# Finer pieces at both ends, small products on GpSimd, and more of TensorE's waits in the plan of an attention and FFN kernel

## The chip, the cores and the metric

The kernel runs on one core of a Trainium2 chip. The metric is the device time of one execution in microseconds. The core has five engines that run side by side, each in the order in which its instructions were written: TensorE (PE) multiplies matrices into PSUM, ScalarE (ACT) computes activations, VectorE (DVE) does arithmetic on tensors, GpSimd (POOL) does arithmetic on SBUF only, and SyncE (SP) issues DMAs. PEld is TensorE's load of weights, which has rows of its own in the profile.

## The reference, cut to what matters

Sizes: S = 2048 rows, D = 512, H = 32 heads of 16, F = 1792; data in bf16.

```
g = sigmoid((x * gate_w).sum(-1, keepdims=True))
q, k, v = split(x @ wqkv)                       # 32 heads of 16
a = concat(softmax(q @ k.T * 16**-0.5) @ v) @ wo
b = (silu(x @ w_gate) * (x @ w_up)) @ w_down
out = g * a + (1 - g) * b
```

## The kernel before, in words

**Tiles.** The queries are cut into 4 blocks of 512 (qb), the heads into 8 groups of 4 (g). One block with one group is a unit, 32 in all (UNIT, line 117), and a unit has 16 key tiles of 128. One key tile of a unit, in the text a tile, has 4 heads, so it is four score banks of 128 keys x 512 queries in PSUM: 512 tiles, 2048 banks. The 8 PSUM banks are shared by all work.

**Two ways to an exponential.** A score bank becomes a probability either on ScalarE (`emit_group`: one ACTIVATE with Exp over two banks, sometimes three, into `e_all`), or on VectorE (`emit_d`): a TENSOR_SCALAR turns the fp32 score into the bits of a number (tile `c_t`, or a home in `wd_t` or `kaug`), and further cheap operations on the whole 2048 columns of the tile improve it. These are either two bit operations and one product (`bits`, `product`, group size 2) or three shifted copies (`copy`, group size 4). GpSimd takes over some of the copies and of the products in pieces (`lifted`, `beside`, `take_over`). Each result is a moving operand of the multiplication with v (`pv`), so a tile of VectorE costs TensorE two or four such multiplications, and one of ScalarE one.

**The order is written out by a planner.** The Python code that emits the instructions keeps a clock for each engine (`Plan`: pe, dve, act, pool), advances it by fixed costs (`spend` for TensorE, `spend_v` for VectorE), and picks the next instruction by scores whose weights stand in `WEIGHTS`, changed at about 60 given slots of the run. The split of the tiles between ScalarE and VectorE comes out of the same choice (`choose`, `v_unit`). The chip does not see the plan, only the order on each engine and the semaphores between engines. `later` queues work for VectorE, and `fill_dve` decides when it goes out; the flag `fast` marks operations that read SBUF only. `beside(span)` gives GpSimd work when the next operations of VectorE read PSUM; a dependency ties each such GpSimd instruction behind the last `fast` VectorE instruction before it.

**Side work** (qkv projections, the FFN, output projections) comes in chains of pieces (`Chain`, `Pacer`), each with a release slot and a deadline; `force` empties a chain that is due. `q_pieces` makes the query operand of two groups: a copy out of PSUM (`qst`), its magnitude `aq`, the product of `aq` with the bound of the keys `kb` (`weigh`), and 2 x 8 DMAs on the SP queue.

**End of a unit.** `post` copies the sum over the keys out of PSUM into `osb` and adds a tiny number to the denominators' rows. `settle` sends the rows to `onc` and the denominators to DRAM. `recip`, once for each query block, loads the denominators as `dn`, inverts them, spreads them as `rb` by DMA, and multiplies each of the blocks of `onc` by `rb` (`norm`; 4 blocks for the first three query blocks, 3 for the last).

**Both ends.** At the start (from line 1560 on) the first keys (`kp0`, two banks) and queries (`qp0`) are projected; the largest key magnitude (`largest`, `k_neg`) makes a bound that is added to the queries (`bound_add`), and two masked variants of the queries (`q0a`) feed the first scores. At the end the last unit's sum is copied by ScalarE, its denominators are collected (`denominators`), inverted, spread over the rows (`spread_rows`), multiplied in (`on_l`), and the last product with wo goes into four banks (`a_ps`) that already hold the rest of the output; `last_pieces` and `tail` make that rest.

## Time and profile before

| | us |
|---|---|
| median of 3 runs | 751.14 (750.82 to 751.19) |
| profiled execution, its time | 751.17 |
| span from its first to its last instruction | 749.4 |
| first exponential of scores begins | 13.44 |
| last exponential of scores ends | about 740.6 |

The profile comes from one execution. All positions in it are microseconds from the start of the span, and 1.77 us of the profiled execution lie outside it. The helpers record all instructions of TensorE under line 260, of ScalarE under 263 and of VectorE, GpSimd and SP under 275, so groups are told apart by their tiles. The busy time of a group counts an overlap of two instructions of one engine once, and the mean is of single instructions, which overlap their neighbours: two VectorE instructions of 0.68 us each can begin 0.60 us apart. The spacing of the beginnings is what an instruction costs its engine.

### The profile page before, as it was taken

The page shows a single profiled execution, that of the slowest core. Times are in us where ns is not written, and L with a number is a line of the kernel's source. Part 1 is how long each engine was busy: PE and PEld are TensorE (multiplying, and loading weights), DVE is VectorE, ACT ScalarE, POOL GpSimd, SP SyncE. Part 2 cuts the span into 40 slices and gives each one's busy share as a digit, 9 for nine tenths or more (in the row PEclk, how much of TensorE's full clock was granted, in tenths as well). Part 3 has the DMA queues.
Part 4 walks back from the last instruction along what each step waited for, and adds up shares of the span by engine and source line. Part 5 has one row for each costly group of instructions (what it writes and reads, how often), then busy time and mean ns, then how long its engine had stood idle before and what let it go on. Part 6 is the DMA issues. An engine that isn't in the chain of part 4 may idle for free.

```text
span 749.4 us, 23683 instructions
## 1 busy us (share of the span) xinstructions
PE 733.1 (98%) x10009; PEld 237.0 (32%) x10009; DVE 724.2 (97%) x1196; ACT 733.5 (98%) x827; POOL 246.2 (33%) x342
## 2 busy tenths in 40 slices
PE   7999999999999999999999999999999999999997
PEld 3333332333332333333333233233333333332332
DVE  6799999999999999999999999999999999999995
ACT  5999999999999999999999999999999999999996
POOL 5142030442534443531443322553113403403221
PEclk9999999999999999999999999999999999999999
DMA  9000212344210003220200041312000231200001
GB/s 211 23 2 16 51 32 42 72 121 101 49 36 13 20 24 82 58 53 21 59 16 11 25 109 31 70 27 60 18 23 16 62 82 42 47 19 14 14 31 36
DMA packets 91025, 34.48 MB, mean 46 GB/s; under 512 B 75488, under 2 KB 90472, under 8 KB 90920
## 3 DMA queue, kind: packets, MB, share of 16 engines
q1 hardware_dynamic: 89192, 32.66, 18.5%
q8 instruction: 78, 1.28, 0.7%
q10 hardware_dynamic: 1728, 0.33, 0.3%
q14 instruction: 27, 0.22, 0.1%
HBM read 21.55 MB, written 2.35 MB: 32 GB/s over the span
## 4 chain that ended last, share of the span: by engine, by line
ACT 70%; PE 24%; DVE 4%; issue 2%; DVEq 0%
ACT e_all L263 66%; PE psum L260 24%; ACT th L263 3%; DVE c_t L275 2%; DVE mt L275 0%; DVE gs L275 0%; DVE kaug L275 0%; ACT mt L263 0%; ACT xT L263 0%; DVE rd L275 0%; ACT osb L263 0%; DVE osb L275 0%; DVE o_t L275 0%; DVE qx L275 0%; DVE rn L275 0%
## 5 line engine op out<-in xcount | busy, mean ns | idle before, releaser
L263 ACT ACTIVATE e_all<-psum 128x1024 bf16<-128x1024 f32 x758 | 709.7, 1126 | 1.2 <-PE psum L260 1.0
L275 DVE TENSOR_SCALAR c_t<-psum 128x512 uint16<-128x512 f32 x443 | 295.4, 686 | 4.4 <-PE psum L260 3.3
L260 PE MATMUL psum<-qx,kaug 32*128 32x512 bf16 (+1 forms) x1632 | 250.3, 385 | 6.0 <-ACT e_all L263 4.4
L275 POOL TENSOR_TENSOR c_t<-c_t,lift 128x256 int32<-128x256 int32 (+2 forms) x152 | 105.7, 702 | 274.5 <-DVE c_t L275 216.3
L260 PE MATMUL psum<-e_all,vaug 128*32 128x512 bf16 (+3 forms) x2032 | 169.5, 330 | 0.0
L260 PEld LDWEIGHTS <-kaug 32*128 32x128 bf16 (+1 forms) x2048 | 76.3, 91 | 268.8 <-ACT e_all L263 195.7
L260 PEld LDWEIGHTS <-vaug 128*32 128x32 bf16 x4012 | 96.8, 95 | 125.1 <-issue 88.4
L260 PE MATMUL psum<-c_t,vaug 128*32 128x512 bf16 (+3 forms) x1712 | 132.9, 337 | 0.5 <-DVE mt L275 0.2
L275 DVE TENSOR_SCALAR c_t<-c_t 128x2048 uint16<-128x2048 uint16 (+1 forms) x191 | 129.8, 686 | 0.9
L275 POOL TENSOR_TENSOR c_t<-c_t 128x512 bf16<-128x512 bf16 (+2 forms) x54 | 49.7, 933 | 84.8 <-DVE c_t L275 45.8
L260 PE MATMUL psum<-wd_t,mt 128*32 128x512 bf16 x896 | 73.4, 382 | 0.0
L260 PE MATMUL psum<-xT,wg 128*32 128x512 bf16 x896 | 72.6, 384 | 0.0
L260 PE MATMUL psum<-xT,wu 128*32 128x512 bf16 x896 | 71.7, 383 | 0.4 <-DVE c_t L275 0.3
L275 DVE TENSOR_TENSOR c_t<-c_t 128x2048 bf16<-128x2048 bf16 (+1 forms) x42 | 50.9, 1213 | 0.0
L260 PE MATMUL psum<-q,kaug 32*128 32x512 bf16 (+1 forms) x256 | 50.1, 385 | 0.5 <-ACT e_all L263 0.2
L275 DVE TENSOR_SCALAR kaug<-psum 128x512 uint16<-128x512 f32 (+1 forms) x67 | 44.8, 687 | 0.8 <-PE psum L260 0.4
L260 PE MATMUL psum<-xT,wqk 128*32 128x512 bf16 x512 | 40.9, 383 | 0.0
L263 ACT ACTIVATE th<-psum 128x512 bf16<-128x512 f32 x56 | 38.8, 693 | 0.0
L275 DVE SCALAR_TENSOR_TENSOR gs<-th,psum 128x512 bf16<-128x512 bf16 x56 | 37.9, 676 | 0.4 <-ACT th L263 0.3
L275 DVE SCALAR_TENSOR_TENSOR mt<-gs,psum 128x512 bf16<-128x512 bf16 x56 | 37.9, 677 | 0.3
L275 POOL TENSOR_TENSOR kaug<-c_t,lift 128x256 int32<-128x256 int32 (+1 forms) x31 | 21.1, 681 | 50.3 <-DVE c_t L275 33.2
L275 POOL TENSOR_TENSOR c_t<-kaug,lift 128x256 int32<-128x256 int32 (+1 forms) x30 | 20.7, 697 | 40.1 <-DVE c_t L275 19.7
(124 smaller groups left out, 464.0 us busy)
## 6 DMA issues: line engine op xcount, KB each, us to landing
wg<-in_B_w_gate_dram SPq DMA_DIRECT2D x56, 128.0 KB
wu<-in_B_w_up_dram SPq DMA_DIRECT2D x56, 128.0 KB
on<-osb SPq DMA_DIRECT2D x120, 16.0 KB
rb<-rr SPq DMA_DIRECT2D x15, 128.0 KB
wd_t<-in_B_w_down_dram SPq DMA_DIRECT2D x7, 256.0 KB
qx<-qst SPq DMA_DIRECT2D x96, 16.0 KB
qx<-aq SPq DMA_DIRECT2D x96, 16.0 KB
out_dram<-o_t SPq DMA_DIRECT2D x12, 128.0 KB
```

Of the source, the lines that this page charges most:

```text
L260: return ordered(nc.tensor.matmul(out, lhsT=lhsT, rhs=rhs, **kw), [lhsT, rhs], [out])
L263: ordered(nc.scalar.activation(out=out, in_=in_, **kw), [in_, *kw.values()], [out])
L275: return ordered(f(*a, **kw), [v for v in (*a, *kw.values()) if v is not out], [out])
```

## The change

Five groups of edits.

**Start.** The keys' projection runs bank by bank instead of alternating, each bank has its own maximum (`largest(0)`, `largest(3)`) and its own copy to `kaug`; the queries are made in two halves of 256 columns in two banks (`qp0` and `warm`), and VectorE evicts the one half while ScalarE evicts the other.

**GpSimd.** `weigh` (16 products) and `norm` of the first three query blocks (12 products) are made by GpSimd in pieces of 256 columns, through a new list `asides` that `beside` serves ahead of the tile's own work. The tiny number is added to `dn` once for each query block, by GpSimd (a new list `guarded`, on which `spread` waits); so `post` makes a plain copy for 29 of the 32 units.

**Planner.** New constants for TensorE (FLIP, UNIT_US, PIECE_US, COLS_US, TURN); score groups begin no earlier than the query chain's planned end, multiplications with v no earlier than their operands' planned ends, the `parts` chain no earlier than its ratio. These alter the order only, they add no semaphore.

**Weights.** EB, FACE, OWN, LATEST and all entries of `WEIGHTS` have new values, with LATEST as a 27th of each entry.

**End.** The last unit's copy, denominators, inversion and spreading go in two halves; the rest of the output is made by four chains of five column pieces, one for each 128 rows (`last`), which the pacer can place from 8, 6, 4 and 2 slots before the end.

The diff, without the weights:

```diff
-    FLIP, UNIT_US, PIECE_US, COLS_US = 0.097, 0.224, 0.011, 0.213
+    FLIP, UNIT_US, PIECE_US, COLS_US, TURN = 0.1055, 0.2157, 0.0024, 0.2133, 0.0105
...
             def mag():
...
-                plan.chain = me
-                later(0.21, weigh, plan.dve, ("q", b), fast=True)
-
-            def weigh():
-                vec.tensor_scalar(out=aq[:, :], in0=aq[:, :], scalar1=kb[:, b:b + 1], scalar2=None, op0=ALU.mult)
-                rows(aq, DH)
+                aside(weigh, QBW, lambda: rows(aq, DH), me)
+
+            def weigh(cols):
+                return gps.tensor_tensor(out=aq[:, cols], in0=aq[:, cols], in1=kb[:, b:b + 1].broadcast_to([P, QBW // 2]), op=ALU.mult)
...
-        start = max(plan.pe + (FLIP if plan.mode != "R" else 0.0), rel)
+        start = max(plan.pe + (FLIP if plan.mode != "R" else 0.0), rel,
+                    *(q_of[b // 4 // KT].t_done for b in bs if b // 4 // KT in q_of))
...
+    def aside(f, width, done=None, chain=None):
+        if chain is not None:
+            chain.owed += 1
+        asides.append([plan.dve + 0.1, f, width, 0, done, chain])
+
+    def aside_now():
+        job = asides[0]
+        _, f, width, k, done, c = job
+        ins = f(slice(k, k + min(width, QBW // 2)))
+        if fast_last[0] is not None:
+            tc.add_manual_dep(ins.ins, fast_last[0].name,
+                              mybir.DependencyInfo(mybir.DependencyClass.Sync, mybir.DependencyReason.DATA), reason="beside reads of PSUM")
+        plan.pool = max(plan.pool, plan.dve + POOL_IN) + POOL_FIX + 0.48
+        job[3] = k + QBW // 2
...
     def beside(span):
 
         if plan.pool > plan.dve + 0.05:
             return
+        if asides and asides[0][0] <= plan.dve and span + POOL_OVER - POOL_IN - POOL_FIX >= POOL_ONE:
+            aside_now()
+            return
...
         elif un == UNITS - 1:
-            act(out=osbs[un][:, :], in_=o[:, :], func=ACT.Identity, bias=tiny[:, 0:1], scale=1.0)
+            for cs in (slice(0, QBW // 2), slice(QBW // 2, QBW)):
+                act(out=osbs[un][:, cs], in_=o[:, cs], func=ACT.Identity, bias=tiny[:, 0:1], scale=1.0)
         else:
-            vec.tensor_scalar(out=osbs[un][:, :], in0=o[:, :], scalar1=tiny[:, 0:1], scalar2=None, op0=ALU.add)
+            if un == UNITS - 2:
+                vec.tensor_scalar(out=osbs[un][:, :], in0=o[:, :], scalar1=tiny[:, 0:1], scalar2=None, op0=ALU.add)
+            else:
+                vec.tensor_copy(out=osbs[un][:, :], in_=o[:, :])
...
+        guarded = []
+        at.setdefault(n0 + 4, []).append(lambda: aside(
+            lambda cols: gps.tensor_tensor(out=dn[0:4 * n, :], in0=dn[0:4 * n, :], in1=tiny_row[0:4 * n, :].broadcast_to([4 * n, P]), op=ALU.add),
+            P, lambda: guarded.append(0)))
+
         def spread():
+            while not guarded:
+                aside_now()
+            plan.dve = max(plan.dve, plan.pool)
...
-            at.setdefault(n0 + 13 + b, []).append(lambda norm=norm: later(0.345, norm, fast=True))
+            if full:
+                def product(cols, b=b):
+                    return gps.tensor_tensor(out=onc[qb][:, b, cols], in0=onc[qb][:, b, cols], in1=rb[:, b, cols], op=ALU.mult)
+                at.setdefault(n0 + 13 + b, []).append(lambda b=b, product=product: aside(product, QBW, lambda: normed.add((qb, b))))
+            else:
+                at.setdefault(n0 + 13 + b, []).append(lambda norm=norm: later(0.345, norm, fast=True))
...
-    def last_pieces():
+    def last_pieces(tq):
...
+        return columns(NB + 1, "al", lambda i: last_rows(tq)(i)[0], lambda i: last_rows(tq)(i)[1], keep, stop=False)
...
-    for dc in arrived:
-        for tb in range(2):
+    for tb in range(2):
+        for dc in arrived:
             mm(kp0[:, tb * QBW:(tb + 1) * QBW], lhsT=wpad[1][:, dc, :], rhs=xT[:, dc, tb * QBW:(tb + 1) * QBW],
                start=(dc == arrived[0]), stop=(dc == arrived[-1]))
-    for dc in arrived:
-        mm(qp0[:, :], lhsT=wpad[0][:, dc, :], rhs=xT[:, dc, 0:QBW], start=(dc == arrived[0]), stop=(dc == arrived[-1]))
-    largest(0, kp0[:, :])
+    HW = QBW // 2
+    halves = [(qp0[:, 0:HW], slice(0, HW)), (warm[:, 0:HW], slice(HW, QBW))]
+    for p, cs in halves:
+        for dc in arrived:
+            mm(p, lhsT=wpad[0][:, dc, :], rhs=xT[:, dc, cs], start=(dc == arrived[0]), stop=(dc == arrived[-1]))
+    largest(0, kp0[:, 0:QBW])
     k_neg(kneg1, 0, idle[:, 0:P])
-    act(out=aq0, in_=qp0[:, :], func=ACT.Abs)
-    act(out=kaug[:, 0, 0:2 * QBW], in_=kp0[:, :], func=ACT.Identity, bias=onescol[:, 0:1], scale=1.0)
-    vp0 = v0(0)
-    bound_add(qp0, kneg1, aq0)
-    vec.tensor_scalar(out=q0a[:, 0, :], in0=qp0[:, :], scalar1=vsel[:, 0:1], scalar2=None, op0=ALU.mult)
-    act(out=q0a[:, 1, :], in_=qp0[:, :], func=ACT.Identity, scale=vsel[:, 1:2])
+    largest(3, kp0[:, QBW:2 * QBW])
+    k_neg(kneg1, 3, kneg1)
+    act(out=kaug[:, 0, 0:QBW], in_=kp0[:, 0:QBW], func=ACT.Identity, bias=onescol[:, 0:1], scale=1.0)
+    for p, cs in halves:
+        act(out=aq0[:, cs], in_=p, func=ACT.Abs)
+    act(out=kaug[:, 0, QBW:2 * QBW], in_=kp0[:, QBW:2 * QBW], func=ACT.Identity, bias=onescol[:, 0:1], scale=1.0)
+    vp0 = m_tile("vp")
+    v0(vp0, range(3))
+    for p, cs in halves:
+        bound_add(p, kneg1, aq0[:, cs])
+    v0(vp0, range(3, 8))
+    for v in range(2):
+        vec.tensor_scalar(out=q0a[:, v, halves[0][1]], in0=halves[0][0], scalar1=vsel[:, v:v + 1], scalar2=None, op0=ALU.mult)
+        act(out=q0a[:, v, halves[1][1]], in_=halves[1][0], func=ACT.Identity, scale=vsel[:, v:v + 1])
...
+    for tq in range(TQ):
+        last.append(pace.add(last_pieces(tq), SLOTS - (KT // 2, 6, 4, 2)[tq], SLOTS + tq, downs, cond=ripe, begun=last[-1:]))
...
+    for h in range(2):
+        dt = m_tile("dt")
+        denominators(dt, osb, (2 * h, 2 * h + 1))
+        rts.append(work.tile([P, 4 * TQ], BF16, tag="rt", name="rt"))
+        recip16(rts[h][:, 8 * h:8 * h + 8], dt[:, 8 * h:8 * h + 8])
+    tail(1)
+    for h in range(2):
+        rps = m_tile("rps")
+        spread_rows(rps, rts[h], (2 * h, 2 * h + 1))
+        for tq in (2 * h, 2 * h + 1):
+            cs = slice(tq * P, (tq + 1) * P)
+            vec.tensor_tensor(out=on_l[:, cs], in0=osb[:, cs], in1=rps[:, cs], op=ALU.mult)
```

More of the change, by code (lines that the diff above doesn't have):

```diff
@@ L402 @@
     owed = []
+    asides = []
     work_at = []
@@ L1560 @@
     ratio_done = []
+    differs = []
     part_scaled = []
@@ L1605 @@
+    vec.tensor_copy(out=v0_out(0), in_=vp0[:, :].rearrange("p (t h c) -> p t h c", h=4, c=DH))
+    for p, cs in halves:
+        vec.tensor_copy(out=q0_bf[0][:, cs], in_=p)
+    m_free(vp0, plan.pe + 1.0)
+    m_free(qp0, plan.pe + 1.6)
+    m_free(warm, plan.pe + 2.0)
     for g in (3, 4):
@@ L1659, with scaled_by @@
     v_late = pace.add(v0_pieces(8), 2, 5, [known])
-    parts = pace.add(columns(1, "rp", lambda k: sbc_t, lambda k: ratio, scale_part), 3, 11, [again], 1,
-                     cond=lambda: part_done and ratio_done)
+    def scaled_by(k):
+        plan.pe = max(plan.pe, ratio_done[0])
+        return ratio
+    parts = pace.add(columns(1, "rp", lambda k: sbc_t, scaled_by, scale_part), 3, 11, [again], 1,
+                     cond=lambda: part_done and ratio_done and (plan.slot >= 14 or plan.pe >= ratio_done[0]))
     need[6] = [again]
@@ L2053 @@
             continue
-        if closed == UNITS - 1 and pv_left(closed) <= 2 and not a_ps[2:]:
-            tail_ready()
-            tail(3)
         next_pv()
     for c in sorted(pace.chains, key=lambda c: c.deadline):
-        force(c)
+        if c not in last:
+            force(c)
     while owed:
```

179 lines of the change are left out of this document (96 added, 83 removed).

## The prediction

> **What bounds the kernel now.** I read the busy time of the engines first, then the same by stretch, then the costliest groups, then the chain that ended last, and at the end both ends of the timeline.
>
> ```profile
> PE 733.1 (98%) x10009; PEld 237.0 (32%) x10009; DVE 724.2 (97%) x1196; ACT 733.5 (98%) x827; POOL 246.2 (33%) x342
> ACT 70%; PE 24%; DVE 4%; issue 2%; DVEq 0%
> ```
>
> Three engines are busy nearly all the time, and only GpSimd (POOL) has room. In the windows view each engine's busy time follows the stretch and its length, in the order PE, PEld, DVE, ACT, POOL. This row runs from the first exponential to the end of the last:
>
> ```profile
> 13.44:740.64 727.20, 718.00 (x9889) 230.44 (x9889) 713.78 (x1158) 726.04 (x817) 235.47 (x314) 1.00 0.18 44
> ```
>
> From the first exponential at 13.44 to the last at 740.64 ScalarE is idle for 727.20 - 726.04 = 1.2 us, VectorE for 727.20 - 713.78 = 13.4 us. ScalarE's busy time could still hide waits, since its instructions overlap. So I look at what an exponential costs when nothing holds it up, in the chain:
>
> ```profile
> 671.59 33.00 ACT e_all L263 x36
> ```
>
> That is 0.917 us each. The page's groups give the number:
>
> ```profile
> L263 ACT ACTIVATE e_all<-psum 128x1024 bf16<-128x1024 f32 x758 | 709.7, 1126 | 1.2 <-PE psum L260 1.0
> L275 DVE TENSOR_SCALAR c_t<-psum 128x512 uint16<-128x512 f32 x443 | 295.4, 686 | 4.4 <-PE psum L260 3.3
> L275 DVE TENSOR_SCALAR c_t<-c_t 128x2048 uint16<-128x2048 uint16 (+1 forms) x191 | 129.8, 686 | 0.9
> L275 DVE TENSOR_TENSOR c_t<-c_t 128x2048 bf16<-128x2048 bf16 (+1 forms) x42 | 50.9, 1213 | 0.0
> L263 ACT ACTIVATE th<-psum 128x512 bf16<-128x512 f32 x56 | 38.8, 693 | 0.0
> 117.37 0.49 ACT th L263
> ```
>
> 758 x 0.917 + 56 x 0.49 = 722.5 us of the 727.2: the 4.7 us left over hold the four wider exponentials and small operations too. **ScalarE is the bound, and nothing but fewer exponentials on it shortens the middle.** A tile costs it two instructions, 2 x 0.917 = 1.83 us. The other place for a tile is VectorE, which is itself 98% busy there. So the price of the middle is VectorE's work: what is taken from VectorE can be spent on tiles taken from ScalarE.
>
> **The rate of that exchange.** Spacings of beginnings show what an operation costs VectorE:
>
> ```profile
> 285.07 0.68 DVE L275 TENSOR_SCALAR c_t<-c_t 128x2048 uint16<-128x2048 uint16 x1
> 285.67 1.22 DVE L275 TENSOR_TENSOR c_t<-c_t 128x2048 bf16<-128x2048 bf16 x1
> 286.81 0.68 DVE L275 SCALAR_TENSOR_TENSOR gs<-th,psum 128x512 bf16<-128x512 bf16 x1
> 299.31 0.67 DVE L275 CAST qst<-psum 128x512 bf16<-128x512 f32 x1
> 299.91 0.67 DVE L275 TENSOR_SCALAR c_t<-psum 128x512 uint16<-128x512 f32 x1
> ```
>
> A read of PSUM and a bit operation or copy take 0.60 us, a product 1.14. The 443 reads are 443 / 4 = 110.75 tiles; with 191 copies and bit operations and 42 products a tile costs (443 x 0.60 + 191 x 0.60 + 42 x 1.14) / 110.75 = 3.9 us. If s us are taken from VectorE's work and the middle shrinks by x, then x / 1.83 tiles move, and VectorE has x less time as well: s = x + 3.9 x / 1.83, so **x = s / 3.13**. The bounds of a tile's price are 4 x 0.60 = 2.4 (GpSimd makes all copies) and 2.4 + 1.2 + 1.14 = 4.74 (none), which give s / 2.3 and s / 3.6.
>
> **What GpSimd takes off VectorE.** The products and the copies that change, with their spacing:
>
> ```profile
> L275 DVE TENSOR_TENSOR on<-on,rb 128x512 bf16<-128x512 bf16 x15 | 6.4, 431 | 0.0
> L275 DVE TENSOR_SCALAR aq<-aq,kb 128x512 bf16<-128x512 bf16 x16 | 6.1, 382 | 0.0
> L275 DVE TENSOR_SCALAR osb<-psum,tiny 128x512 bf16<-128x512 f32 x30 | 22.2, 740 | 0.0
> 293.84 0.45 DVE L275 TENSOR_TENSOR on<-on,rb 128x512 bf16<-128x512 bf16 x1
> 294.21 0.74 DVE L275 TENSOR_SCALAR osb<-psum,tiny 128x512 bf16<-128x512 f32 x1
> 294.87 0.45 DVE L275 TENSOR_TENSOR on<-on,rb 128x512 bf16<-128x512 bf16 x1
> 301.31 0.34 DVE L275 TENSOR_SCALAR aq<-aq,kb 128x512 bf16<-128x512 bf16 x1
> 301.57 0.68 DVE L275 TENSOR_SCALAR c_t<-psum 128x512 uint16<-128x512 f32 x1
> ```
>
> Twelve of the 15 normalising products at 294.21 - 293.84 = 0.37 are 4.4 us; 16 weighing products at 0.26 are 4.2; 29 copies lose 294.87 - 294.21 - 0.60 = 0.06 each, 1.7. Together s = 10.3 us. GpSimd gets 28 x 2 = 56 pieces of 256 columns and four guards of 128. Its nearest row, and one place where its work meets VectorE's:
>
> ```profile
> L275 POOL TENSOR_TENSOR c_t<-c_t 128x256 bf16<-128x256 bf16 x26 | 17.3, 672 | 25.0 <-DVE c_t L275 15.5 <-PE psum L260 8.0 <-DVE wd_t L275 1.6
> 290.62 0.61 POOL L275 TENSOR_TENSOR c_t<-c_t,lift 128x256 int32<-128x256 int32 x1 [10.29 <-DVE c_t L275]
> 291.00 0.79 DVE L275 TENSOR_SCALAR c_t<-kaug 128x2048 uint16<-128x2048 uint16 x1
> 291.71 0.68 DVE L275 TENSOR_SCALAR c_t<-psum 128x512 uint16<-128x512 f32 x1
> ```
>
> 56 x 0.67 = 38 us on an engine that is idle for 727 - 235 = 492 us of the middle: that is the cover, and pieces of the tiles' work that come one slot later cost nothing while a slot is free. The stretch is the price. The GpSimd piece ended at 291.23; the operation of VectorE on SBUF alone that had begun at 291.00 took 0.71 to its successor instead of 0.60. A 0.67 us piece would stretch such a successor by 0.11 + 0.06 = 0.17. A successor on SBUF alone is likely about 3 times in 10 (191 + 42 such rows stand against 443 reads, and evictions and gating add to the reads). I take 56 x 0.17 x 0.3 = 2.9 us; the ends are 0 and 56 x 0.17 = 9.5. So s = 7.4 and **x = 2.4 us**, between 0.3 and 3.3. The weighing operand is one broadcast column in fp32, which no GpSimd row shows; the int32 pieces with a broadcast operand take 0.61, so I keep 0.67 and carry a slow one into a rival. The Trainium skill ("GPSIMD Engine Reference", opening section) calls GpSimd the wrong choice for ordinary elementwise arithmetic, about 2x behind VectorE. By that, the products lose time; the rows agree on the ratio and more, 0.67 against 0.37 / 2, but the time lost is that of an idle engine.
>
> Downstream of the moved steps: the eight DMAs of each `aq` now wait on SP for GpSimd instead of VectorE, and the loads of `wg` and `wu` stand behind them. The query chain is forced 12 slots ahead of its use, some 17 us by 727 / 512 us a slot, against a delay of two pieces; I cost it at nothing, and a microsecond on SP has the same cover. The guard stands between the landing of `dn` and its reciprocal, on which VectorE would wait in order; it is issued three slots earlier, 4 us, for at most 0.6 us of work. Without that cover it is 4 x 0.6 us of VectorE, 0.8 us of time.
>
> **The start.** The path to the first exponential runs through one reduction over two banks:
>
> ```profile
> 7.93 2.75 PE L260 MATMUL psum<-xT,mt 128*128 128x512 bf16 x12 [0.45 <-ACT xT L263]
> 9.86 1.23 DVE L275 TENSOR_REDUCE kpart<-psum 128x1 f32<-128x1024 f32 x1 [1.49 <-PE psum L260]
> 11.12 0.35 DVE L275 SCALAR_TENSOR_TENSOR mt<-mt,kpart 128x128 bf16<-128x128 bf16 x1
> 12.06 0.75 DVE L275 TENSOR_SCALAR mt<-psum,vsel 128x512 bf16<-128x512 f32 x1 [0.59 <-PE psum L260]
> 12.85 0.69 ACT L263 ACTIVATE mt<-psum,vsel 128x512 bf16<-128x512 f32 x1 [0.53 <-DVE mt L275]
> 16.33 0.63 DVE L275 TENSOR_REDUCE kpart<-psum 128x1 f32<-128x512 f32 x1
> ```
>
> A matmul takes 2.75 / 12 = 0.23. With the banks in turn the first four end at 9.0, and reduction and bound follow (0.63 + 0.35) to 10.0; the second bank is ready at 9.9, and its two operations end at 11.0 instead of 11.47, 0.5 us earlier. The first variant is then evicted in halves side by side, some 0.45 each instead of 0.75, but ScalarE's half has to queue behind three copies. I let the halves win nothing on the first variant, so the first exponential comes 0.5 us earlier, and give 0.1 for the second variant (ScalarE's 0.69 at 12.85 was in front of the second pair of scores). **0.6 us**, between 0 and 1.0.
>
> **The end.** After the last exponential:
>
> ```profile
> 740.44 0.82 PE L260 MATMUL psum<-wo_t,on 128*128 128x512 bf16 x3
> 741.19 0.62 PE L260 MATMUL psum<-e_all,vaug 128*32 128x512 bf16 x8
> 741.86 0.69 ACT L263 ACTIVATE osb<-psum,tiny 128x512 bf16<-128x512 f32 x1 [1.21 <-PE psum L260]
> 743.77 0.88 DVE L275 TENSOR_TENSOR on_l<-osb,psum 128x128 bf16<-128x128 bf16 x4 [0.62 <-PE psum L260]
> 744.65 1.41 DVE L275 TENSOR_SCALAR mt<-psum,gval 128x512 bf16<-128x512 f32 x2
> ```
>
> Output products at 740.44 stand ahead of the last multiplications with v; as pieces of 0.22 they hold them up by one piece, not three: 0.2 us, if the plan sees it. The first half of the copy is ready some 0.2 earlier than 0.69, its inversion and spreading run beside the second half, and the four products of 0.22 begin up to 0.4 earlier; VectorE's first eviction at 744.65 waits for them. I take 0.4, together **0.6 us**, between -0.3 (more instructions, each with its semaphore) and 1.0.
>
> **The new order.** The planner's edits and weights add no instruction of their own. What they can win is VectorE's idle 13.4 us, 13.4 / 3.13 = 4.3 us of time at most; what they can lose is as much, by a split that costs more. The row of the first stage says where idle time is:
>
> ```profile
> 13.44:100.00 86.56, 84.64 (x1137) 26.98 (x1136) 80.34 (x143) 86.11 (x96) 20.79 (x32) 1.00 0.19 45
> ```
>
> 6.2 of the 13.4 us lie before 100, where VectorE has little to take. A plan whose waits are nearer to the chip's should regain part of the rest: I take 5 us of the 13.4, **1.6 us**. This is the term with the least behind it.
>
> **Sum.** 751.17 - 2.4 - 0.6 - 0.6 - 1.6 = 746.0 us. The profiled execution is 0.03 us from the median, so it stands for the runs as well. A repeat of runs differs by up to 0.4 us, and 0.2%, 1.5 us, is about what a measurement can tell from no change.
>
> **Rivals.** *Only the ends gain.* The split stays: VectorE's freed time becomes idle time because no home or bank is free for more tiles. For it speaks that VectorE already leaves 13.4 us unused; against it, that these are mostly in the first stage. Time: 751.17 - 1.2 = 750.0. *The new order fills VectorE.* The whole idle time goes, there is no stretch, and the ends give 1.2: 751.17 - 4.3 - 3.3 - 1.2 = 742.4. For it: ScalarE's row shows no other limit. Against it: the chain is held by TensorE for 24%, and a tile on VectorE costs TensorE one to three multiplications more. *GpSimd holds VectorE up*, which ends on the other side. Place: the 56 pieces. If a piece overlaps a whole operation of VectorE on SBUF, or the fp32 column makes it twice as long, VectorE loses up to 0.60 a piece: 56 x 0.60 = 33.6, (33.6 - 10.3) / 3.13 = 7.4 us more, less 1.2 at the ends: 757.4. It decides from 0.25 us a piece, where 56 x 0.25 = 10.3 + 1.2 x 3.13. For it speaks the 0.79 us row; against it that the overlap there was a tail of 0.23 us. The Trainium skill ("SBUF — State Buffer", Who interferes with whom) states that the shared pair of ports is locked for a whole instruction and the loser fully blocks. The trace agrees as far as the 0.79 row goes; the dependency behind the last SBUF operation is what keeps the overlap to tails.
>
> **Chances.** The forecast 0.47 (744 to 748.5), the filled VectorE 0.26, only the ends 0.13, GpSimd in the way 0.14. The range, 742.0 to 751.0, leaves out the last and a little of the second. Faster by over 0.2%, below 749.6: 0.73; within: 0.13; slower: 0.14.
>
> **What the profile after would show.** The exponentials' count falls from 758 to about 754 (2.2 tiles for 4.0 us); ScalarE stays idle for under 2 us of the middle; the first exponential begins near 12.9; the rows `on<-on,rb` on VectorE fall to 3, and `aq<-aq,kb` goes to GpSimd with 32 pieces of 0.61 to 0.67; GpSimd's busy time rises by about 38 us; from the last exponential to the end of the span are 8.2 us instead of 749.40 - 740.64 = 8.8. I am wrong if the count of exponentials stays or rises, if ScalarE begins to wait, or if bit operations of VectorE grow beyond 0.79.

## The result and the profile after

| | before | after |
|---|---|---|
| median, us | 751.18 (750.74 to 751.68) | 749.43 (749.14 to 750.66) |
| ratio of the medians | | 0.9979, interval 0.9972 to 0.9986 |
| profiled execution, its time and span | 751.17, 749.4 | 750.66, 748.9 |
| first exponential begins | 13.44 | 12.87 |
| from the first exponential to the end of the last | 727.2 | 728.3 |
| from there to the end of the span | 8.8 | 7.7 |

The change wins 1.75 us, with an interval of 1.1 to 2.1. The forecast was 5.1. By the profiles it lies at the two ends: 0.6 us ahead of the first exponential and 1.1 us behind the last. The middle, where the forecast had put 4.0, gives nothing.

The page of the kernel after, busy time of the engines and the shares of the chain that ended last:

```profile
PE 728.0 (97%) x10047; PEld 236.3 (32%) x10047; DVE 716.7 (96%) x1174; ACT 734.0 (98%) x824; POOL 276.2 (37%) x397
ACT 60%; PE 21%; DVE 12%; issue 3%; SPq 2%; DMA 1%; DVEq 0%
```

VectorE has lost 7.5 us of work and GpSimd has got 30 (its new pieces are more, 19.4 + 15.8 us below; it does less for the tiles); ScalarE is where it was. The windows view (stretch, its length, then busy time of PE, PEld, DVE, ACT, POOL) for the middle, and its part from 100 to 740:

```profile
12.87:741.20 728.33, 714.58 (x9916) 229.57 (x9918) 706.01 (x1133) 725.85 (x809) 265.48 (x368) 1.00 0.18 43
...
100.00:740.00 640.00, 629.61 (x8764) 202.28 (x8756) 627.33 (x990) 639.63 (x716) 241.84 (x333) 1.00 0.19 44
```

ScalarE's 725.85 stands against 726.04 before. VectorE's fell from 713.78 to 706.01, so 7.8 us were freed, and its idle time in the middle rose from 13.4 to 728.33 - 706.01 = 22.3 us (21.5 in a second profile of this kernel). The freed time was not used.

The groups of the kernel after, shapes kept apart (busy time and mean ns of one, then idle time before them):

```profile
L263 ACT ACTIVATE e_all<-psum 128x1024 bf16<-128x1024 f32 x731 | 685.4, 1102 | 2.6 <-PE psum L260 2.5
L276 DVE TENSOR_SCALAR c_t<-psum 128x512 uint16<-128x512 f32 x438 | 289.3, 682 | 8.0 <-PE psum L260 6.2
L276 DVE TENSOR_SCALAR c_t<-c_t 128x2048 uint16<-128x2048 uint16 x180 | 124.4, 698 | 1.4 <-PE psum L260 0.7
L263 ACT ACTIVATE e_all<-psum 128x1536 bf16<-128x1536 f32 x19 | 27.8, 1541 | 0.0
L276 POOL TENSOR_TENSOR aq<-aq,kb 128x256 bf16<-128x256 bf16 x32 | 19.4, 613 | 40.9 <-DVE c_t L276 38.9 <-DVE kaug L276 1.4 <-DMA qx<-qst 0.6
L276 POOL TENSOR_TENSOR on<-on,rb 128x256 bf16<-128x256 bf16 x24 | 15.8, 669 | 37.6 <-DVE c_t L276 28.6 <-DVE kaug L276 8.3 <-DVE aq L276 0.7
L276 DVE TENSOR_TENSOR on<-on,rb 128x512 bf16<-128x512 bf16 x3 | 1.2, 417 | 0.0
L263 ACT ACTIVATE e_all<-psum 128x512 bf16<-128x512 f32 x1 | 0.8, 760 | 0.0
```

and the two rows of the kernel before that are needed beside them:

```profile
L263 ACT ACTIVATE e_all<-psum 128x1024 bf16<-128x1024 f32 x754 | 704.7, 1124 | 1.2 <-PE psum L260 1.0
L263 ACT ACTIVATE e_all<-psum 128x1536 bf16<-128x1536 f32 x4 | 5.8, 1470 | 0.0
```

The number of exponentials did fall, from 758 to 751, more than forecast, and that sign misleads. Counted in score banks it is 754 x 2 + 4 x 3 = 1520 before and 731 x 2 + 19 x 3 + 1 = 1520 after: 380 tiles on ScalarE both times. There are more of the three-bank form, not fewer tiles.

The start and the end of the kernel after, from its timeline:

```profile
9.20 0.69 DVE L276 TENSOR_REDUCE kpart<-psum 128x1 f32<-128x512 f32 x1 [1.15 <-PE psum L260]
...
12.87 5.60 ACT L263 ACTIVATE e_all<-psum 128x1024 bf16<-128x1024 f32 x6 [0.16 <-PE psum L260]
...
18.95 0.39 PE L260 MATMUL psum<-xT,wqk 128*32 128x512 bf16 x2 [1.32 <-DMA wqk<-in_A_wqkv_dram]
...
19.70 1.02 ACT L263 ACTIVATE e_all<-psum 128x1024 bf16<-128x1024 f32 x1 [1.23 <-PE psum L260]
...
741.72 0.84 ACT L263 ACTIVATE osb<-psum,tiny 128x256 bf16<-128x256 f32 x2 [0.52 <-PE psum L260]
...
743.38 0.88 DVE L276 TENSOR_TENSOR on_l<-osb,psum 128x128 bf16<-128x128 bf16 x4 [0.32 <-PE psum L260]
...
744.17 1.40 DVE L276 TENSOR_SCALAR mt<-psum,gval 128x512 bf16<-128x512 f32 x2
```

The first reduction begins 0.66 us earlier than before, the first exponential 0.57. At 18.95 TensorE waits 1.32 us for a load of weights, and ScalarE with it, 1.23 us up to 19.70. A second profile of this kernel has 0.5 us there, and four profiles of the runs below with this start and order have none (products back, more work for ScalarE, more for TensorE, pieces left out), so this wait varies between executions; it is as long as the 1.2 us by which the profiled execution is above the median, and it makes the middle 1.1 us longer than before. Without it the middle is 727.1 us, the 727.2 of before. The kernel before begins this projection at 19.86 instead of 17.24 and doesn't meet the wait. At the end ScalarE waits 0.52 instead of 1.21 us for the last sums with v, and from the beginning of its copy to the first eviction are 2.45 us instead of 2.79.

### The profile page after: what moved, and what is told of

It is laid out like the page before. It is cut to its first block, busy times and chain, and to the rows that moved or that the text cites. A ratio compares the mean times of both kernels' runs of the same rounds, so it can differ in the third digit from the quotient of the medians.

```text
span 748.9 us, 23842 instructions
## 1 busy us (share of the span) xinstructions
PE 728.0 (97%) x10047; PEld 236.3 (32%) x10047; DVE 716.7 (96%) x1174; ACT 734.0 (98%) x824; POOL 276.2 (37%) x397
## 4 chain that ended last, share of the span: by engine, by line
ACT 60%; PE 21%; DVE 12%; issue 3%; SPq 2%; DMA 1%; DVEq 0%
ACT e_all L263 56%; PE psum L260 21%; DVE c_t L276 8%; ACT th L263 3%; SPq L276 2%; DVE kaug L276 1%; DVE mt L276 1%; DMA wqk<-in_A_wqkv_dram 1%; DVE gs L276 1%; DMA on<-osb 1%; DVE osb L276 0%; ACT mt L263 0%; DVE qst L276 0%; DVE rd L276 0%; ACT osb L263 0%
## 5 line engine op out<-in xcount | busy, mean ns | idle before, releaser
L263 ACT ACTIVATE e_all<-psum 128x1024 bf16<-128x1024 f32 (+1 forms) x751 | 709.1, 1113 | 2.6 <-PE psum L260 2.5
L260 PE MATMUL psum<-qx,kaug 32*128 32x512 bf16 (+1 forms) x1632 | 246.2, 385 | 7.3 <-ACT e_all L263 6.6
L276 POOL TENSOR_TENSOR c_t<-c_t,lift 128x256 int32<-128x256 int32 (+1 forms) x175 | 121.0, 700 | 180.0 <-DVE c_t L276 123.4
L276 DVE TENSOR_SCALAR c_t<-c_t 128x2048 uint16<-128x2048 uint16 x181 | 124.6, 696 | 1.4 <-PE psum L260 0.7
L276 POOL TENSOR_TENSOR c_t<-c_t 128x256 bf16<-128x256 bf16 (+2 forms) x65 | 54.8, 858 | 97.9 <-DVE c_t L276 79.1
L276 DVE TENSOR_SCALAR kaug<-psum 128x512 uint16<-128x512 f32 x76 | 50.9, 682 | 1.4 <-PE psum L260 0.8
L276 DVE TENSOR_TENSOR c_t<-c_t 128x2048 bf16<-128x2048 bf16 (+1 forms) x36 | 43.7, 1214 | 0.0
L276 POOL TENSOR_TENSOR aq<-aq,kb 128x256 bf16<-128x256 bf16 x32 | 19.4, 613 | 40.9 <-DVE c_t L276 38.9
L260 PEld LDWEIGHTS <-mt 128*32 128x32 bf16 (+1 forms) x1045 | 24.0, 95 | 29.1 <-issue 21.2
```

What stands on the lines that cost most here:

```text
L260: return ordered(nc.tensor.matmul(out, lhsT=lhsT, rhs=rhs, **kw), [lhsT, rhs], [out])
L263: ordered(nc.scalar.activation(out=out, in_=in_, **kw), [in_, *kw.values()], [out])
L276: return ordered(f(*a, **kw), reads, [out])
```

## The experiments

The prediction's theory: VectorE's work is the price of the middle, because its time can be turned into tiles taken from ScalarE. The rivals: the order and the split on the chip are fixed, so freed VectorE time is idle time; GpSimd's new pieces cost VectorE what they save it; the ends are lost or found elsewhere. Expectations name theories by number or letter; each text says what they are. A run's own kernel before, timed on the same chip, is 751.38 for the first four, 750.87 for the next four, 751.1 for two and 751.37 for the last three. The kernel after is 749.3 beside the first four, ratio 0.9977 (0.9968 to 0.9986); I take it as 749.1 beside the next four, by the same ratio.

**The change again.** No edit.

> The changed kernel again, for times on the same chip as the others and a second profile. If the wait of 1.2 us on ScalarE near 18 us (TensorE waiting for the load of wqk) belongs to single executions, this profile's middle is about 727 us between the first and the last exponential, and the time is 749.4. If it belongs to the order, the wait is there again.

749.3 us, span 748.3, first exponential at 12.86, 7.75 us behind the last. The wait is there again, but shorter, 0.5 us; the middle is 727.7 us, 727.2 without it.

**The ends alone.** Kernel before, in its order, with the new start and with the halves at the end; the output products stay whole.

```diff
 (start and end of the kernel after, in the kernel before; these lines against the kernel after)
+    m_free(vp0, 0.0)
+    m_free(warm, 0.0)
-    m_free(vp0, plan.pe + 1.0)
-    m_free(warm, plan.pe + 2.0)
```

> The kernel before with the change's start and with the halves at the end (copy, denominators, inversion, spreading), everything else and the order of the middle as before; the output products stay where they were. Theory 1 (only the ends gained): the traces give 0.57 us at the start and 0.34 us behind the last copy, so 750.3, ratio 0.9988. Theory 2 (the middle gained as well and gave some back): the start's 0.57 us would be lost again because the order of the middle is written for other times, so 750.7 or more.

751.54 us, ratio 1.0003 (0.9994 to 1.0012): no gain. This kernel tests less than it was meant to. In its profile the first exponential is 0.9 us earlier, at 12.53, but the third waits:

```profile
12.53 1.02 ACT L263 ACTIVATE e_all<-psum 128x1024 bf16<-128x1024 f32 x1 [0.16 <-PE psum L260]
...
13.62 0.38 PE L260 MATMUL psum<-mt,kaug 32*128 32x512 bf16 x1 [0.83 <-DVE mt L276]
...
13.93 2.55 PE L260 MATMUL psum<-xT,mt 128*32 128x512 bf16 x24
...
17.06 1.02 ACT L263 ACTIVATE e_all<-psum 128x1024 bf16<-128x1024 f32 x1 [2.00 <-PE psum L260]
```

Two things add up here. The bank `warm` still holds half of the queries while the plan thinks it free, so TensorE waits 0.83 us for the copy; that is of my making, not the change's. And the 24 multiplications behind it take 2.55 us, where the kernel before takes 1.48:

```profile
13.91 1.48 PE L260 MATMUL psum<-xT,mt 128*32 128x512 bf16 x24
```

In this execution the granted clock of TensorE (the value before the last two) was 0.50 just there:

```profile
14.19:17.60 3.41, 3.41 (x34) 0.86 (x26) 2.71 (x4) 1.41 (x2) 0.00 (x0) 0.50 1.06 320
```

It is also the slowest of this kernel's 11 executions, 1.3 us above their median, and the median one shows a clock of 1.0, so the median does not hold this second part. The 1.56 us by which an early exponential is late here are still 1.6 at the last one. The end can be read all the same: 8.9 us behind the last exponential, against 8.8 before. The halves alone win nothing, probably since two products of the rest still stand whole in front of the spreading on TensorE. The time is in theory 2's range, but with these waits it doesn't tell the theories apart.

**The products back.** Kernel after, its order untouched, the 28 products on VectorE again.

```diff
-                return gps.tensor_tensor(out=aq[:, cols], in0=aq[:, cols], in1=kb[:, b:b + 1].broadcast_to([P, QBW // 2]), op=ALU.mult)
+                return vec.tensor_scalar(out=aq[:, :], in0=aq[:, :], scalar1=kb[:, b:b + 1], scalar2=None, op0=ALU.mult)
...
-                    return gps.tensor_tensor(out=onc[qb][:, b, cols], in0=onc[qb][:, b, cols], in1=rb[:, b, cols], op=ALU.mult)
+                    return vec.tensor_tensor(out=onc[qb][:, b, :], in0=onc[qb][:, b, :], in1=rb[:, b, :], op=ALU.mult)
```

> The changed kernel with its 28 weighing and normalising products back on VectorE at the same places of its order; nothing else moves. VectorE has 8.6 us more to do (16 x 0.26 + 12 x 0.37). Theory 1 (380 tiles stay on ScalarE, whose work sets the middle; what VectorE saved became idle time): under 2 us more than the changed kernel, 749.5 to 751.5. Theory 2 (VectorE's time counts one to one in a fixed order): 5 to 8.6 us more, 754.5 to 758.

753.9 us, ratio 1.0036 (1.0024 to 1.0049): 4.6 us above the change for 8.6 us of work (by the distance between beginnings; VectorE's busy time in the middle rose by 711.5 - 706.2 = 5.3 us over the change run again). Neither theory had this size. An order made for less VectorE work doesn't bear its return, but that says nothing yet of what taking it away is worth.

**More work for ScalarE.** Kernel after, 50 small exponentials added.

```diff
+                count[0] += 1
+                if count[0] % 15 == 0:
+                    act(out=extra_out[:, :], in_=xT[:, 0, 0:96], func=ACT.Exp, scale=inv_sqrt_dh)
```

> The changed kernel with one small Exp of 96 columns more behind every 15th exponential of scores, about 50 in all, which the plan does not know; nothing reads their output. They should take ScalarE 0.14 to 0.20 us each, 7 to 10 us. Theory 1 (ScalarE sets the middle): the time rises by 80 to 100% of what they take, to 756 or more. Theory 2 (VectorE or TensorE sets it): by less than half of it, 753 at most.

756.11 us, ratio 1.0061 (1.0049 to 1.0074): 6.8 us above the change for about 8.5 us of work (0.17 us each), 80% of it, the lower end of theory 1.

**More work for TensorE.** Kernel after, 39 multiplications with zeros added, each as long as one with v.

```diff
+        if un in o_of and pvs[un] and un and pv_left(un) > 1:
+            more[0] += 1
+            if more[0] % 23 == 0:
+                for j in range(4):
+                    mm(o_of[un][32 * j:32 * j + 16, :], lhsT=vaug[:, 0, G * 4 * VC:], rhs=xT[:, 0, 0:QBW],
+                       start=False, stop=False, tile_position=(0, 32 * j), skip_group_check=True)
```

> The changed kernel with one multiplication of zeros more (four column matmuls, about 0.22 us of TensorE) in front of every 23rd multiplication with v, some 30 in all, 6 to 7 us, which the plan does not know. Theory 1 (ScalarE sets the middle and TensorE has slack): the time rises by less than a third of it, 751.5 at most. Theory 2 (TensorE sets the middle as well, so that what VectorE saved could not be used): by two thirds or more, 753.5 or above.

754.35 us, ratio 1.0045 (1.003 to 1.006): 5.2 us above the change for 8.4 us of work (there were 39 of them, not some 30). That is 62%, just short of theory 2's two thirds and far from theory 1. Added work costs on each of the three engines.

**The old weights.** Kernel after with the weights of before (EB, OWN and FACE with them).

```diff
-    WEIGHTS = {8: (0.351, 2, 6.286, ...
+    WEIGHTS = {8: (0.107, 2, 8.063, ..., 0.64), ...
```

> The changed kernel's code with the weights of the kernel before (LATEST 0.64 throughout), so that the order is planned anew with weights that were not found for this code. The plan keeps 384 tiles on ScalarE instead of 380 and ends 11.8 us later. Theory 1 (the order that the weights give decides the middle): 759 to 763. Theory 2 (the weights hardly matter on the chip, waits fill up): within 3 us of the changed kernel.

761.86 us, ratio 1.0148 (1.0134 to 1.0162): 12.7 us above the change, as theory 1 had it. The same code with less VectorE work gives 757 x 2 + 7 x 3 + 1 = 1536 banks to ScalarE, 384 tiles:

```profile
L263 ACT ACTIVATE e_all<-psum 128x1024 bf16<-128x1024 f32 x757 | 705.9, 1094 | 3.6 <-PE psum L260 3.3
L276 DVE TENSOR_SCALAR c_t<-psum 128x512 uint16<-128x512 f32 x432 | 287.3, 683 | 18.1 <-PE psum L260 17.0
...
L263 ACT ACTIVATE e_all<-psum 128x1536 bf16<-128x1536 f32 x7 | 9.9, 1549 | 0.0
```

In the code of before these weights gave 380 tiles. So the split follows from the weights and the code together, and with the weights held, less VectorE work moved it the wrong way. In this code the new weights are worth more than any other part of the change; what they would do in the code of before no run shows.

**The products moved in the old order.** Kernel before, the 28 products given to GpSimd where they stood, not beside VectorE's reads of PSUM.

```diff
-                vec.tensor_scalar(out=aq[:, :], in0=aq[:, :], scalar1=kb[:, b:b + 1], scalar2=None, op0=ALU.mult)
+                on_pool(lambda cols: gps.tensor_tensor(out=aq[:, cols], in0=aq[:, cols], in1=kb[:, b:b + 1].broadcast_to([P, QBW // 2]), op=ALU.mult))
```

> The kernel before with its 16 weighing products and 12 of its 15 normalising products moved to GpSimd in pieces of 256 columns, at the same places of the order, with the plan's clocks as before. The mirror of the run with the products back on VectorE. Theory 1 (in a fixed order with 380 tiles on ScalarE freed VectorE time turns into idle time): 0 to 1 us less than before, 750.4 to 751.4. Theory 2 (VectorE's time counts in a fixed order by about half, as 4.6 of 8.6 us in the other run): 4 us less, 747.4.

755.59 us, ratio 1.0061 (1.0049 to 1.0074): 4.6 us slower than before. Neither theory had a loss. One place in its timeline shows how it comes:

```profile
296.69 1.29 POOL L275 TENSOR_TENSOR on<-on,rb 128x256 bf16<-128x256 bf16 x2
...
297.95 1.15 POOL L275 TENSOR_TENSOR c_t<-kaug,c_t 128x512 bf16<-128x512 bf16 x1
298.01 1.64 DVE L275 TENSOR_SCALAR c_t<-c_t 128x2048 uint16<-128x2048 uint16 x1
299.06 1.06 POOL L275 TENSOR_TENSOR c_t<-c_t,lift 128x256 int32<-128x256 int32 x1
...
300.17 0.29 PE L260 MATMUL psum<-c_t,vaug 128*32 128x256 bf16 x3 [1.61 <-POOL c_t L275]
...
300.82 1.02 ACT L263 ACTIVATE e_all<-psum 128x1024 bf16<-128x1024 f32 x1 [1.58 <-PE psum L260]
```

Two products of GpSimd push its own piece of a tile to 297.95, where it meets a bit operation of VectorE. That takes 1.64 us instead of the usual 0.68 (0.78 at this place before), and the copy behind it, 256 columns, 1.06 instead of 0.61. TensorE then waits 1.61 us for GpSimd, and ScalarE 1.58 us for TensorE. Over the whole run the exponentials' idle time is 4.8 us against 1.2:

```profile
L263 ACT ACTIVATE e_all<-psum 128x1024 bf16<-128x1024 f32 x758 | 710.2, 1126 | 4.8 <-PE psum L260 4.4
```

Exponential by exponential, this place makes the run 1.8 us later than the kernel before. Right behind it the granted clock was 0.50 for 3.4 us (from 301.8) in this execution, during which the exponentials fall another 1.2 behind; three of the five executions have a mean clock of 1.0 and are not faster. At a second place two products again stand in front of GpSimd's own piece, for another 0.8 us; the rest of the 4.6 comes in smaller steps:

```profile
420.26 1.18 POOL L275 TENSOR_TENSOR aq<-aq,kb 128x256 bf16<-128x256 bf16 x2
...
421.41 0.61 POOL L275 TENSOR_TENSOR kaug<-c_t,lift 128x256 int32<-128x256 int32 x1
...
422.07 0.38 PE L260 MATMUL psum<-kaug,vaug 128*32 128x512 bf16 x1 [0.45 <-POOL kaug L275]
...
422.81 1.95 ACT L263 ACTIVATE e_all<-psum 128x1024 bf16<-128x1024 f32 x2 [0.66 <-PE psum L260]
```

VectorE's bit operations grew a little, from before to this run:

```profile
L275 DVE TENSOR_SCALAR c_t<-c_t 128x2048 uint16<-128x2048 uint16 x188 | 129.0, 692 | 0.9
...
L275 DVE TENSOR_SCALAR c_t<-c_t 128x2048 uint16<-128x2048 uint16 x188 | 131.6, 706 | 0.9
```

VectorE's whole busy time is 722.3 us, against 724.2 before and 718.6 with the products left out (below). So GpSimd holds VectorE up by some 3.7 us, which is less than it frees, and a fuller VectorE doesn't explain the loss. GpSimd's pieces can cost more than they save, but mainly in another way than the prediction's rival had it: they delay GpSimd's own pieces of the tiles, for which TensorE waits. In the kernel after, where `beside` places them, the pieces cost about 0.5 us (the pieces left out, below); its order differs in more than the placement.

**The old start.** Kernel after with the start of before.

```diff
-    for tb in range(2):
-        for dc in arrived:
+    for dc in arrived:
+        for tb in range(2):
...
-    largest(0, kp0[:, 0:QBW])
+    largest(0, kp0[:, :])
```

> The changed kernel with the start of the kernel before (one reduction over both banks, queries in one bank), the rest of the order as it is. If the earlier start reaches the end, it costs the 0.57 us that the first exponential comes later: 749.9. If the order behind it waits for something else (a load, a bank) at about 18 us, nothing: 749.3.

750.03 us, ratio 0.9988 (0.9979 to 0.9996). That is 0.9 us above the change's 749.1, with intervals that overlap, so the times make it likely but don't show it. The profiles say more. Here the first exponential begins at 13.21, in the run without the pieces (below; same order, new start) at 12.94, neither waits for the load, and the 0.27 us between them are still 0.34 at the 400th exponential: what the start wins is carried on. The wait for the load can take it back, though. In the second profile of the change the first exponential is 0.35 us earlier than here, and the last ends at 740.54 against 740.52.

**The products left out.** Kernel before, its order untouched, without the 28 products and with nothing in their place.

```diff
-                vec.tensor_scalar(out=aq[:, :], in0=aq[:, :], scalar1=kb[:, b:b + 1], scalar2=None, op0=ALU.mult)
                 rows(aq, DH)
...
+                if not full:
                     vec.tensor_tensor(out=onc[qb][:, b, :], in0=onc[qb][:, b, :], in1=rb[:, b, :], op=ALU.mult)
```

> The kernel before with the 16 weighing and 12 normalising products left out (the output is not the reference's); nothing takes their place on GpSimd, the order and everything else stay. VectorE has 8.6 us less to do. Theory 1 (in a fixed order, whose split keeps 380 tiles on ScalarE, freed VectorE time turns into idle time): 0 to 1 us less than the kernel before. Theory 2 (freed time counts by half, as added time did): 4 to 5 us less, 746.5.

751.05 us, ratio 0.9998 (0.9989 to 1.0007): 8.6 us of VectorE's work taken away, and no gain, as theory 1 had it. The windows row of its middle and the group that waits:

```profile
13.28:740.30 727.02, 717.56 (x9888) 230.11 (x9889) 708.20 (x1130) 725.85 (x817) 234.98 (x314) 1.00 0.18 44
```

```profile
L275 DVE TENSOR_SCALAR c_t<-psum 128x512 uint16<-128x512 f32 x443 | 296.1, 687 | 7.8 <-PE psum L260 5.8 <-POOL c_t L275 0.2
```

VectorE is idle for 727.02 - 708.20 = 18.8 us instead of 13.4. That is 5.4 more and not 8.6, for 8.6 counts distances between beginnings, and busy time fell by 5.6 only: probably the ends of instructions that a product used to overlap now count as busy. Its reads of scores wait for TensorE 5.8 us instead of 3.3. It finishes early and stands before the next score bank.

**The pieces left out.** Kernel after without GpSimd's 56 pieces; the four guards stay.

```diff
-        ins = f(slice(k, k + min(width, QBW // 2)))
-        if fast_last[0] is not None:
+        ins = f(slice(k, k + min(width, QBW // 2))) if width < QBW else None
+        if ins is not None and fast_last[0] is not None:
```

> The changed kernel with the 56 GpSimd pieces of the weighing and normalising products left out (the output is not the reference's), the order and the four guards stay. It shows what the pieces cost beside the PSUM reads. The rows before gave 0.17 us of VectorE for a piece whose successor works on SBUF, 2.9 us of VectorE in all. Theory 1 (VectorE has idle time and the pieces lie beside reads): 0 to 0.5 us less than the changed kernel. Theory 2 (GpSimd holds VectorE up, and that ate the gain of the middle): 2 us less or more.

748.91 us, ratio 0.997 (0.9959 to 0.9981), 0.5 us below the change by the ratios, less than their intervals, and in theory 1's range. The bit operations, VectorE's work on SBUF alone:

```profile
L276 DVE TENSOR_SCALAR c_t<-c_t 128x2048 uint16<-128x2048 uint16 x180 | 123.8, 694 | 1.4 <-PE psum L260 0.7
```

Their mean is 694 ns, with the pieces 698, and VectorE's whole busy time is 715.8 us, with them 716.7. Beside reads of PSUM the pieces are nearly free.

**Relief for ScalarE, for TensorE, for all three.** What was open now was whether ScalarE alone is the bound. Three kernels from the kernel before, in its order. The first narrows every 14th exponential, the second leaves out every 12th multiplication with v, the third does both and leaves out the 28 products.

```diff
+                count[0] += 1
+                cw = QBW - 96 if count[0] % 14 == 0 and count[0] > 28 else QBW
-                act(out=e_all[:, e0:e0 + w, :], in_=psum[:, p[0]:p[0] + w, :], func=ACT.Exp, scale=inv_sqrt_dh)
+                act(out=e_all[:, e0:e0 + w, 0:cw], in_=psum[:, p[0]:p[0] + w, 0:cw], func=ACT.Exp, scale=inv_sqrt_dh)
...
+        skip = False
+        if un and not first and not last and c1 - c0 == QBW:
+            less[0] += 1
+            skip = less[0] % 12 == 0
```

> The kernel before, its order untouched, with ScalarE relieved: 52 of its exponentials (every 14th from the 28th on) compute 2 x 416 columns instead of 2 x 512. 1541 ns for three banks against 1102 for two make 0.86 ns a column, so 192 columns fewer are 0.165 us and all of them 8.6 us. The left-out columns hold old numbers. Theory A, the prediction's reading (ScalarE alone is the bound and nothing but its work sets the middle): the time falls by 7 to 8.6 us, to 742.5 to 744. Theory B (in a fixed order three engines are the bound by turns, so relief of one is caught by the next): it falls by 1 to 4 us.

748.58 us, ratio 0.9968 (0.9955 to 0.998): 2.8 us for 8.6, as theory B had it. The shares of the chain turn over, from ScalarE's 70% to

```profile
PE 50%; ACT 27%; DVE 19%; issue 2%; DMA 1%; DVEq 0%
```

> The kernel before, its order untouched, with TensorE relieved: every 12th whole multiplication with v that is neither the first nor the last of its unit is left out, 39 of them at 0.216 us, 8.4 us, about what the relief of ScalarE is in the run beside it. The sums lack those tiles. Theory A (ScalarE alone is the bound): no change beyond 0.7 us. Theory B (three engines by turns): the time falls by 1 to 4 us.

751.04 us, ratio 0.9997 (0.9988 to 1.0005): nothing for 8.4, as theory A had it.

> The kernel before with all three reliefs at once: ScalarE 8.6 us less (narrower exponentials), TensorE 8.4 us less (39 multiplications with v left out), VectorE 8.6 us less (28 products left out). Theory A (ScalarE alone is the bound): what the relief of ScalarE alone gives, within 1 us. Theory B (three engines by turns): more than the sum of the three single reliefs, 6 to 8.6 us, so 742.5 to 745.

746.61 us, ratio 0.9941 (0.9927 to 0.9954): 4.8 us. That is more than the 2.8 + 0.3 + 0.0 of the single reliefs, though at the edge of the noise, more than theory A allowed, and less than theory B's 6. Its chain:

```profile
ACT 44%; PE 44%; DVE 9%; issue 2%; DMA 0%; DVEq 0%
```

Together:

| engine | relieved, us of work | time | loaded, us of work | time |
|---|---|---|---|---|
| VectorE | 8.6 | 0.0 | 8.6 | +4.6 |
| TensorE | 8.4 | -0.3 | 8.4 | +5.2 |
| ScalarE | 8.6 | -2.8 | 8.5 | +6.8 |
| all three | 8.4 to 8.6 each | -4.8 | | |

The reliefs are of the kernel before, the loads of the kernel after; each kernel keeps its order, and each time has an interval of some 0.7 to 1.2 us to either side. In the order of the kernel before ScalarE is the first bound. With it relieved, the chain stands on TensorE for half of the span, so TensorE is likely the next; ScalarE and TensorE relieved without VectorE were not run, so VectorE's part of the 4.8 is not told apart. What relief one engine gets, the others take back; what load one engine gets, the others wait for. Why the three reliefs together stop at 4.8 is open. They do not fall at the same places of the run, which would explain a part; I did not try them at the same places.

## Why the prediction was wrong, step by step

**The step that failed** is the exchange, "what is taken from VectorE can be spent on tiles taken from ScalarE", with x = s / 3.13 = 2.4 us, and with it the 1.6 us of the new order, which rests on the same turning of idle VectorE time into tiles. In their place the runs show 0: the tiles on ScalarE are 380 before and after, the middle lasts 727.2 us and, without the wait for the load, 727.1. Two things were wrong in it. First, freed time moves no tile by itself: the split comes out of the planner's choice under its weights, and the changed code had 384 tiles on ScalarE with the old weights and 380 with the new. Without a move, 8.6 us of VectorE are worth nothing (the products left out). Second, a microsecond of ScalarE is not a microsecond of time, at least in the order of the kernel before: relief of 8.6 us gave 2.8, and the chain then stood on TensorE, to which a tile on VectorE gives more to do. What it is in an order made anew for fewer tiles no run shows.

The prediction's bound on ScalarE was too tight as well. Its 0.917 us is 33.00 / 36, with the last one's own end and small waits in it. Over the profile before, the exponentials of two banks begin 0.905 us apart in the median, those of three 1.33, and the 56 of the FFN 0.48, which makes 714 of the 727 us. So up to 13 us are left, not 4.7, in which ScalarE can have waited while its overlapping instructions show it as busy. The rate of the exchange was nearly right: the 443 reads leave out those into `kaug` and `wd_t`, with which 522 of the 528 banks of 132 tiles are found, but the other operations on these tiles were left out too, and the price of a tile comes to 4.0 us instead of 3.9.

The row that could have told it was in the prediction: the chain of before stands on ScalarE for 70%, on TensorE for 24% and on VectorE for 4%. I read the busy shares, 98, 98 and 97%, as three engines with equal claims. The chain's share is nearer to the worth of a small relief: 4% of 8.6 us is 0.3 (measured 0.0), 24% of 8.4 is 2.0 (0.3), 70% of 8.6 is 6.0 (2.8). The shares put the engines in the right order and were too high each time; after the relief of ScalarE the chain had changed hands. For added work they are too low: the 12, 21 and 60% of the chain after give 1.0, 1.8 and 5.1 us against 4.6, 5.2 and 6.8.

**Right in sum, by luck: how much VectorE is freed.** s = 7.4 us was the forecast, 7.8 the measured fall of its busy time in the middle. But the products were put at 8.6, and leaving them out lowers that busy time by 5.6; the stretch was put at 2.9, and leaving the pieces out lowers it by 0.9 (716.7 to 715.8). These two errors go against each other. With the 1.7 of the copies, 5.6 - 0.9 + 1.7 = 6.4 of the 7.8 have a term, and the rest has none. The bit operations, which were to bear the stretch, show 4 ns each, 180 x 0.004 = 0.7 us. The products took 0.61 and 0.67 us a piece on GpSimd, as bounded, and the broadcast fp32 column is the faster of the two. The Trainium skill ("GPSIMD Engine Reference", opening section) has such arithmetic on GpSimd about 2x behind VectorE; here two pieces of 0.613 stand against 0.382, 3.2 times, and the idle engine hid it.

**Right: the start**, 0.57 for 0.6. Single profiles vary: the first exponential begins at 13.21 to 13.51 in the seven with the old start and at 12.18 to 12.94 in the eight with the new one.

**The end, half right.** 1.06 us for 0.6, but the other way round: the output pieces ahead of the last multiplications win 1.21 - 0.52 = 0.69 where I gave 0.2, and the halves 2.79 - 2.45 = 0.34 where I gave 0.4. The halves alone gave nothing (the ends alone, 8.9 us behind the last exponential); the pieces alone were not run. Before, three whole products stood ahead of the last eight multiplications with v, which began at 741.19, 0.55 us behind the end of the exponential. After, all but the last four are done when the exponential ends, and these begin 0.05 us behind it:

```profile
741.25 0.39 PE L260 MATMUL psum<-e_all,vaug 128*32 128x512 bf16 x4
```

**The sum, as it came:** 751.17 - 0.57 - 1.06 = 749.5, beside a median of 749.43. The rival *only the ends gain*, 750.0, is the case that came: VectorE's freed time became idle time, and 12.7 of the 22.3 us lie behind 100, where there were tiles to take. That no home or bank was free for them, the reason it gave, no run shows. *GpSimd holds VectorE up* didn't come. In the old order the products cost 4.6 us, mainly since TensorE waits for GpSimd, but one whole operation of VectorE was held up there as the rival feared. For that the Trainium skill ("SBUF — State Buffer", Who interferes with whom) has the lock for a whole instruction, and the trace agrees: 1.64 us for a 0.68 us operation that began 0.06 us into a piece of 1.15.

**Not settled:** whether another set of weights turns the 22.3 us into fewer tiles on ScalarE. No run here has fewer than 380.

## What to carry to other kernels

Where several engines are over 95% busy, read the worth of freed work from the chain of waits, not from busy time: here VectorE, with 4% of the chain and 97% busy, had nothing to sell, and even the first bound passed on only 2.8 of 8.6 us. In a fixed order freed time became idle time; whether an order made anew turns it into speed hangs on whether the split moves, so count the split (in banks, not in instructions) before believing that it did. The price of added work says little of the worth of taken work: here 4.6 us against 0.

## What the runs showed of the hardware that was not expected

A GpSimd product with a broadcast fp32 column took 613 ns for 256 columns, the plain bf16 one 669. Of 56 such pieces placed beside reads of PSUM the cost was about 0.5 us of time, less than the noise; the same 28 products placed elsewhere, in another order, cost 4.6 us. The load of weights behind the first exponentials is a wait of TensorE of 1.3 us in one execution, of 0.6 in another of the same kernel, and of none in others with the same order. The granted clock of TensorE fell to 0.50 for 3.4 us inside two of the profiles: from 14.2 in the ends alone, 0.6 us behind a wait of TensorE of 0.83 us, and from 301.8 in the products moved, 1.6 us behind one of 1.61. The wait of 1.32 us in the kernel after was followed by no such fall.
